# Who forms the block sums of x, and when GpSimd's other sums may run, in a fused attention and SwiGLU kernel

## The chip, the core and the metric

The kernel runs on one core of a Trainium2 chip. The core has a matrix engine (TensorE, PE in the profile), three engines for elementwise work (VectorE is DVE, ScalarE is ACT, GpSimd is POOL) and a queue that issues most transfers (SyncE, SP). Each engine takes its own instructions in the order in which the program wrote them, and waits at an instruction until what it needs is there. The metric is the device time of one execution in microseconds (us); lower is better. A time here is the median of three executions.

## The reference

Attention over keys and values that are averaged over 8 neighbours, and a gated hidden layer on its result:

```python
# q, k, v: (8 batches, 8 heads, 576, 64); Sp = 72 after averaging over 8
k_p = k.reshape(B, H, Sp, 8, D).mean(axis=3)
v_p = v.reshape(B, H, Sp, 8, D).mean(axis=3)
scores = scale * np.matmul(q, k_p.transpose(0, 1, 3, 2))
scores = scores - np.max(scores, axis=-1, keepdims=True)
attn = np.exp(scores)
attn = attn / (np.sum(attn, axis=-1, keepdims=True) + 1e-09)
x = np.matmul(attn, v_p)          # then heads side by side: (4608, 512)
g = x @ w_gate                    # (512, 1536)
silu = g * (1.0 / (1.0 + np.exp(-g)))
out = (silu * (x @ w_val)) @ w_out   # (1536, 512)
```

## The kernel before

**Tiles and steps.** The 4608 rows of x are taken in 9 tiles of 512 (numbered 0 to 8), the 1536 hidden columns in 12 chunks of 128. All fp32 matrices are split in a high and a low half of 16 bits, and a product is three matmuls (high by high, high by low, low by high). For each tile and chunk there is one step: gate and val (512 to 128) into two PSUM banks `gv`, the gate through a tanh (`hf`, L909 on ScalarE), times itself and times val on VectorE (L913, L919), a high half `hh` (L1279, ScalarE) and a low half `hl` (L1285), and the product with w_out (`project`, L931), which adds to four banks `acc`.

**Plain and fast steps.** In a *plain* step gate and val are each 12 matmuls of 512 columns (`side`, L895 to L897). In a *fast* step gate and val are formed together from 7 products of half blocks, 42 matmuls of 256 columns (`product`, L1015). It needs sums of blocks of the weights (`ws_h`, `ws_l`, made once by `fast_weights`) and of x (`fast_x`, the tiles `fx` and `xc`, made in each tile). READY gives the number of fast steps: 0 in tiles 0 and 1, 5 and 7 in tiles 2 and 3, 9 from tile 4 on. The plain steps stand first in a tile, so from tile 4 on there are 3 plain steps and then 9 steps of 7 products.

**The block sums of x.** `fast_x` runs twice in a tile (once for each j of two): VectorE adds the halves of x to `fx` (L980), GpSimd makes four differences of 128x256 (L982 to L985), ScalarE makes the high half (L989), GpSimd the two low halves `xc` (L991). The first fast step of the tile reads all of it.

**What else the engines do.** While a tile's hidden layer runs, the attention of the next rows is prepared: q is split (GpSimd makes the lows, L591), scores are formed (PE, L608), the largest of each row is taken and subtracted (VectorE, L618, L619), the softmax is made, its halves too (GpSimd, L704 and L707), turned by a DMA transpose (SP, L711), multiplied by v (PE, L732 and L733, from the tile `pt`), divided (VectorE, L737), split and turned once more. For each of the 8 batches there are sums of k, v and q ahead of its rows (`prep`): the v sums over 8 run on GpSimd (L283 to L285, three instructions for each of four pieces), the k sums on VectorE (L278), the largest q on VectorE (L339), each after a load into one of three buffers `mid` (issued at L474). GpSimd also makes `hl` in every fast step, VectorE in the plain steps from tile 2 on.

**What sets the order.** The first tile's order is written out by hand. From then on a planner writes it (`hidden_tiles`): between groups of matmuls `slot` offers room, some ns of VectorE and some of ScalarE (ROOM in plain steps, FAST_ROOM in the others), and each line of waiting work (block sums under the name "extra", then the parts of attention and `prep`) goes forward if its stated need fits. The planner keeps a count of how far PE and each engine are; `spend` adds to it and `settle` holds a line until PE's count is past that of the engine. Three constants belong to the count: LANDS (how long after its issue a load is taken to have landed), TURNS (the same for a transpose) and SETTLE (a margin). The count decides only the order: in the run each engine waits for what it really needs. Of the three `mid` buffers, one was also used for the chunks' weights `wf` in the first tile.

Of the kernel before, what the change touches and what calls it, by code (L numbers as in the profile page):

```python
# [8 lines left out]
F16 = mybir.dt.float16  # L9
F32 = mybir.dt.float32  # L10
# [7 lines left out]
P = 128  # L18
# [39 lines left out]
TILE = 512  # L58
SUB = 128


ROOM = (3500, 3500)
FAST = 9
READY = (0, 0, 5, 7, 9)
FAST_ROOM = (3500, 2700), (2850, 2000), (1550, 750), (950, 0), (2300, 500), (2300, 2000), (2600, 4300)
FAST_FIRST, FAST_THEN = 3, 5
ONE_BANK = (1, 8)
LANDS = 5000
SETTLE = 100
TURNS = 3000  # L70
AHEAD = 9


def _plan(nt, s):
# [17 lines left out]
def attention_then_swiglu(  # L92
# [11 lines left out]
    nc = tc.nc  # L104
    B, _, NJ, S = q.shape
# [4 lines left out]
    DM = NJ * P  # L110
# [45 lines left out]
    wo_h = const.tile([P, NCH, DM], F32R, name="wo_h")  # L156
    wo_l = const.tile([P, NCH, DM], BF16, name="wo_l")
    wo_up = wo_h.bitcast(BF16).rearrange("p c (d t) -> p c d t", t=2)[:, :, :, 1]
    ws_h = const.tile([P, FAST, 3, NJ // 2, P], F16, name="ws_h")
    ws_l = const.tile([P, FAST, 3, NJ // 2, P], F16, name="ws_l")  # L160
    p2w = const.tile([P, NCH, 3], F32, name="p2w")
    ones = const.tile([P, P], F32, name="ones")
    nc.gpsimd.memset(ones, 1.0 / UNIT)
# [12 lines left out]
    inv = const.tile([P, B, 3], F32, name="inv")  # L176
    vst_h, vst_l, vst_f = ([vst[:, 2 * n + i] for i in range(2)] for n in range(3))
    halves = [const.tile([P, 2 * H * P], F16, name=f"half{i}") for i in range(2)]
    zeros = const.tile([P, TILE], F16, name="zeros")

    def fields():
        nc.gpsimd.memset(zeros, 0.0)
# [42 lines left out]
            )  # L225

    def w_abs(c):
        wf = chunks[c]["wf"] = mid.tile([P, 3 * DM], F32, name="wf", tag="mid")
        nc.scalar.activation(wf, chunks[c]["high"].bitcast(F32), AF.Abs, scale=2.0**-112)

    def w_join(c):
# [262 lines left out]
    def prep(b):  # L494

        order = 0, 4, 1, 5, 2, 6, 3, 7
        todo = [i for i in order if ("in", b, i) not in state]

        def load():
            if todo and now["loads"] < 2 and not now["hold"] and now["pe"] >= freed[-3]:  # L500
                batch_load(b, todo.pop(0))

        for i in order:
            while i in todo or state["in", b, i] and now["pe"] < state["from", b, i] + LANDS:
                load()
                yield 0, 0
            for n in (0, 1) if i >= 4 else (None,):
                if state["in", b, i]:
                    yield (batch(b, i)[2], 0, "same") if n else (batch(b, i)[2], 0)
                    batch_sum(b, i, n)  # L510
                    load()
        yield from settle("P")
        mx, ks, vs = state["sizes", b]["t"], home["ks"], home["vs"]
        yield 1300, 0
        nc.vector.tensor_reduce(out=mx[:, 0:1], in_=mx[:, 3:7], axis=AX.X, op=ALU.max)
        largest(mx[:, 1:2], ks)
        largest(mx[:, 2:3], vs)
        yield 0, 0
        yield from settle("V")
        while busy["ps"] or (now["one"] and busy["values"]):  # L520
            yield 0, 0
        busy["sums"] = True
        sums = over_rows(mx[:, :3])
        yield 400, 0
        pow2_above(p2s[:, b, :3], inv[:, b], sums)
        yield from settle("V")
        busy["sums"] = False
        nc.vector.tensor_scalar(
            out=p2s[:, b, 3:4], in0=p2s[:, b, 0:1], scalar1=p2s[:, b, 1:2], scalar2=EXPSCALE,
            op0=ALU.mult, op1=ALU.mult,  # L530
        )
        scaled.add(b)
        while b - 2 in under_way:
            yield 0, 0
        for g in range(2):
            yield (1100, 0, "same") if g else (1100, 0)
            split_k(b, g)
        for g in range(2):
            for part in range(4):
                yield 650, 0, "same"  # L540
                split_v(b, g, part)
        prepped.add(b)
# [2 lines left out]
    now = {"one": False, "job": None, "pe": 0, "V": 0, "A": 0, "P": 0, "loads": 0, "hold": False}  # L545

    def spend(engine, n, *after):
        now[engine] = max(now[e] for e in (engine, "pe", *after)) + n

    def settle(*engines, more=SETTLE):  # L550
        end = max(now[e] for e in engines) + more
        while now["pe"] < end:
            yield 0, 0
# [421 lines left out]
    def fast_x(x, xc):  # L975

        for j in range(HJ):
            yield 1400, 0
            f = xp.tile([P, 2, TILE], F32, name="fx", tag="f", bufs=1)
            nc.vector.tensor_add(f, x["h"][:, j::HJ], x["l"][:, j::HJ])  # L980
            b11, b12, b21, b22 = (f[:, i // 2, i % 2 * HT : (i % 2 + 1) * HT] for i in range(4))
            nc.gpsimd.tensor_sub(b11, b12, b11)  # L982
            nc.gpsimd.tensor_sub(b12, b22, b12)
            nc.gpsimd.tensor_sub(b22, b22, b11)
            nc.gpsimd.tensor_sub(b21, b21, b22)  # L985
            spend("P", 3000, "V")
            yield from settle("P")
            yield 0, 1100
            nc.scalar.copy(xc["h"][:, j], f)  # L989
            for i in range(2):  # L990
                nc.gpsimd.tensor_sub(xc["l"][:, j, i], f[:, i], xc["h"][:, j, i])  # L991
            spend("P", 2400, "A")
            yield from settle("P")

    def product(o, k, c, x, xc, begin):

# [260 lines left out]
    def hidden_tiles():  # L1257
# [41 lines left out]
            return t  # L1299

        def keep_fast(t):
            t["rs"] = hp.tile([P, HT], F32, name="rs")
            nc.scalar.copy(t["rs"], t["r"])
            spend("A", 390)

# [12 lines left out]
        for i, (_, n, _) in list(enumerate(tiles))[1:]:  # L1318
# [25 lines left out]
            for at_step, c in enumerate(order):  # L1344
                now["one"] = now["one"] or (i, c) == ONE_BANK
                ends = at_step == 0, at_step == NCH - 1
                now["hold"] = now["hold"] or ends[1]
                following = order[at_step + 1] if not ends[1] else NCH
                soon = following < ready
                hf = hp.tile([P, TILE], F32, name="hf")[:, :n]  # L1350
                new = None
                if fast:
                    t, gate = fast, fast["gate"]
                    if soon:
                        new = begin_fast(following, x, xc)
                    slot(*FAST_ROOM[2])
                    product(gate[:, HT:], 3, c, x, xc, False)
                    tanh(hf, gate, un, c)
                    slot(*FAST_ROOM[3])
                    product(t["x"], 7, c, x, xc, False)  # L1360
                    nc.scalar.copy(t["r"], t["x"])
                    spend("A", 390)
                    gated(hf, gate)
                    nc.vector.tensor_add(t["x"], t["x"], t["rs"])
                    spend("V", 430)
                    if new:
                        keep_fast(new)

                    def fourth():
                        slot(*FAST_ROOM[4])  # L1370
                        if new:
                            seed_fast(new)
                        slot(*FAST_ROOM[5])
                        product(t["r"], 4, c, x, xc, False)
                        times_val(hf, hf, t["val"], un, c)
                        hh = high_of(hf, n)
                        slot(*FAST_ROOM[6])
                        pending.append((acc, *ends, i, c, hh, low_of(nc.gpsimd, hf, hh, n)))

                    def then():  # L1380
                        if new:
                            second_fast(new, following, x, xc)
                        else:
                            slot(*FAST_ROOM[0])

                    flush({NJ + FAST_FIRST: fourth, NJ + FAST_THEN: then})
                    slot(*FAST_ROOM[1])
                else:
                    gate, val = (gv_bank(g, n) for g in range(2))
                    side(x, c, 0, gate, 0, n, lambda: slot(*ROOM))  # L1390
                    tanh(hf, gate, un, c)
                    gated(hf, gate)
                    slot(*ROOM)
                    side(x, c, 1, val, 0, n, lambda: slot(*ROOM))
                    times_val(hf, hf, val, un, c)
                    hh = high_of(hf, n)
                    slot(*ROOM)
                    hl = low_of(nc.gpsimd if i == 1 else nc.vector, hf, hh, n)
                    if c < later:
                        join("extra", fast_weights(c), ("w", c))  # L1400
                    if soon:
                        new = begin_fast(following, x, xc)
                        keep_fast(new)
                        seed_fast(new)
                    flush({NJ: lambda: slot(*ROOM)})
                    if new:
                        second_fast(new, following, x, xc)
                    slot(*ROOM)
                    pending.append((acc, *ends, i, c, hh, hl))
                fast = new  # L1410
# [62 lines left out]
```

## Time and profile before

| what | us |
|---|---|
| median of three executions | 970.64 |
| lowest, highest | 968.14, 971.66 |
| the profiled execution's own time | 976.08 |
| its span on the core | 973.9 |
| PE idle in the span (973.9 less 925.2 busy) | 48.7 |

The mean clock that TensorE was granted over the profiled execution was 0.982 of full speed. In the rows of the profile a start is in microseconds from the start of the span, the number behind it is the duration, then come engine, line, operation and the tiles written and read; brackets hold how long the engine had been idle before that instruction and what released it. Rows on waits have the total, how often, and the longest.

### The profile page before, as it was taken

To read this page: it belongs to the slowest core of one execution; us is meant where nothing else is said; L and a number is where in the kernel's file an instruction comes from. 1 tells how busy PE (TensorE), PEld (TensorE's weight loads), DVE (VectorE), ACT (ScalarE), POOL (GpSimd) and SP (SyncE) were. 2 spreads that over 40 slices of the span, in tenths; PEclk is the share of its full clock that TensorE was granted. 3 is DMA by queue.
4 is the path that set the end of the run, shared out by engine and by line. 5 is a ranking of instruction groups with operands and counts; after the bars stand their busy time and mean duration, and the time that the engine had idled before them with its cause. 6 is when DMAs were issued, how large, how long until landed. Compare 5 with 4: busy or idle time off the path is not lost. (4 is left out here: it accounts for less than half of the span.)

```text
span 973.9 us, 16809 instructions
## 1 busy us (share of the span) xinstructions
PE 925.2 (95%) x6512; PEld 596.2 (61%) x6512; DVE 625.2 (64%) x1097; ACT 495.8 (51%) x971; POOL 470.2 (48%) x531
## 2 busy tenths in 40 slices
PE   5879999999999999999989999899999999999997
PEld 5657555454555575467647764577567757775775
DVE  5788877768967678767667848475754474233223
ACT  2899883355445446444454455435456454333232
POOL 4433336389659655673484337623534353115111
PEclk9799999999999999999989999899999999999999
DMA  9765436256348214941265226712232322001001
GB/s 351 218 172 199 163 109 170 82 161 163 90 112 206 78 40 80 247 101 28 66 197 142 53 49 176 187 43 57 76 71 55 71 66 65 1 1 44 1 1 44
DMA packets 155535, 103.18 MB, mean 106 GB/s; under 512 B 113216, under 2 KB 141888, under 8 KB 153920
## 3 DMA queue, kind: packets, MB, share of 16 engines
q1 hardware_dynamic: 155456, 102.11, 38.6%
q8 instruction: 51, 0.84, 0.4%
q14 instruction: 28, 0.23, 0.1%
HBM read 67.63 MB, written 9.44 MB: 79 GB/s over the span
## 5 line engine op out<-in xcount | busy, mean ns | idle before, releaser
L1285 POOL TENSOR_TENSOR hl<-hf,hh 128x512 bf16<-128x512 f32 x69 | 90.5, 1312 | 216.4 <-ACT hh L1279 216.2
L931 PE MATMUL acc<-hh,wo_l 128*128 128x512 bf16 (+1 forms) x444 | 169.7, 384 | 0.0
L931 PE MATMUL acc<-hl,wo_h 128*128 128x512 bf16 (+1 forms) x444 | 166.9, 378 | 2.9 <-POOL hl L1285 2.5
L909 ACT ACTIVATE hf<-gv,un 128x512 f32<-128x512 f32 (+1 forms) x111 | 74.9, 675 | 185.1 <-PE gv L1015 118.7
L895 PE MATMUL gv<-x,wgv_h 128*128 128x512 f16 (+1 forms) x432 | 159.6, 370 | 4.5 <-DVE hf L913 2.5
L1279 ACT CAST hh<-hf 128x512 fp32r<-128x512 f32 x96 | 59.4, 619 | 201.7 <-DVE hf L919 201.6
L896 PE MATMUL gv<-x,wgv_h 128*128 128x512 f16 (+1 forms) x432 | 159.4, 369 | 1.3 <-DVE x L747 1.3
L897 PE MATMUL gv<-x,wgv_l 128*128 128x512 f16 (+1 forms) x432 | 159.5, 369 | 0.8 <-DVE wgv_l L264 0.8
L913 DVE SCALAR_TENSOR_TENSOR hf<-hf,gv 128x512 f32<-128x512 f32 (+1 forms) x111 | 74.4, 670 | 124.4 <-ACT hf L909 122.2
L931 PE MATMUL acc<-hh,wo_h 128*128 128x512 f32 (+1 forms) x444 | 133.2, 422 | 0.6 <-ACT hh L1279 0.4
L591 POOL TENSOR_TENSOR box<-qt,box 64x512 f16<-64x512 f32 (+1 forms) x60 | 71.6, 1194 | 109.4 <-ACT box L590 79.8
L1015 PEld LDWEIGHTS <-wgv_h 128*128 128x128 f16 x912 | 88.6, 98 | 37.7 <-issue 6.4
L919 DVE SCALAR_TENSOR_TENSOR hf<-gv,un,hf 128x512 f32<-128x512 f32 x96 | 71.6, 746 | 53.3 <-PE gv L1015 40.0
L1015 PE MATMUL gv<-xc,wgv_h 128*128 128x256 f16 x456 | 81.5, 273 | 10.2 <-POOL xc L991 5.4
L931 PEld LDWEIGHTS acc<-hh,wo_h 128*128 128x128 f32 x444 | 78.3, 193 | 16.6 <-ACT hh L1175 0.9
L1015 PE MATMUL gv<-x,wgv_h 128*128 128x256 f16 x456 | 82.5, 276 | 0.0
L1015 PE MATMUL gv<-xc,ws_h 128*128 128x256 f16 x456 | 80.9, 273 | 0.0
L1015 PEld LDWEIGHTS <-ws_h 128*128 128x128 f16 x684 | 66.5, 98 | 23.4 <-issue 1.9
L931 PEld LDWEIGHTS <-wo_h 128*128 128x128 bf16 x444 | 43.7, 98 | 54.5 <-issue 28.6
L897 PEld LDWEIGHTS <-wgv_l 128*128 128x128 f16 x432 | 42.4, 98 | 49.2 <-issue 2.6
L1314 DVE TENSOR_TENSOR gv<-gv,rs 128x256 f32<-128x256 f32 x57 | 24.6, 432 | 72.0 <-PE gv L1015 66.8
L896 PEld LDWEIGHTS <-wgv_h 128*128 128x128 f16 x432 | 42.4, 98 | 45.2 <-issue 6.3
(173 smaller groups left out, 1942.9 us busy)
## 6 DMA issues: line engine op xcount, KB each, us to landing
ws<-w_all SPq DMA_DIRECT2D x12, 1536.0 KB, 7.1
qt<-q_twice SPq DMA_DIRECT2D x48, 256.0 KB, 2.9
out_t<-ob SPq DMA_DIRECT2D x36, 256.0 KB, 2.5
in<-k_rows SPq DMA_DIRECT2D x12, 576.0 KB, 5.3
in<-q_rows SPq DMA_DIRECT2D x12, 576.0 KB, 5.1
in<-v_main SPq DMA_DIRECT2D x12, 512.0 KB, 4.9
in<-v_rest SPq DMA_DIRECT2D x12, 512.0 KB, 4.5
qt<-q_rows SPq DMA_DIRECT2D x8, 256.0 KB, 3.9
```

What stands on the lines that cost most here:

```text
L591: nc.gpsimd.tensor_sub(o[rows], qt[rows], o[rows])
L895: nc.tensor.matmul(o, wh, x["h"][:, j, a:e], start=(j == 0), stop=False)
L896: nc.tensor.matmul(o, wh, x["l"][:, j, a:e], start=False, stop=False)
L897: nc.tensor.matmul(o, wl, x["h"][:, j, a:e], start=False, stop=(j == NJ - 1))
L909: nc.scalar.activation(hf, gate, AF.Tanh, scale=un[:, c, 0:1])
L913: nc.vector.scalar_tensor_tensor(out=hf, in0=hf, scalar=1.0, in1=gate, op0=ALU.add, op1=ALU.mult)
L919: nc.vector.scalar_tensor_tensor(out=out, in0=val, scalar=un[:, c, 2:3], in1=hf, op0=ALU.mult, op1=ALU.mult)
L931: nc.tensor.matmul(acc[j][:, a:e], w[:, c, j * P : (j + 1) * P], h[:, :n], start=begin and at < NJ, stop=end and w is wo_l,)
L1015: nc.tensor.matmul(o, a, b, start=begin and j + n == 0, stop=j == HJ - 1 and n == 2, skip_group_check=True,)
L1279: nc.scalar.copy(hh[:, :n], hf)
L1285: eng.tensor_sub(hl[:, :n], hf, hh[:, :n].bitcast(F32))
L1314: nc.vector.tensor_add(t["gate"][:, HT:], t["x"], t["rs"])
```

## The change

Five things change. (1) *Numbers of the planner*: ROOM, FAST_ROOM, LANDS (5000 to 6250), SETTLE (100 to 0), TURNS (3000 to 4800), and a factor COST in `spend` that takes GpSimd's stated times at 0.92. (2) *Memory*: `ws_h` and `ws_l` become views of one tile `mixed`, which also holds the chunks' `wf` in the first tile, so that `wf` no longer takes a `mid` buffer; `zeros` moves into a buffer of another pool. (3) *`prep`*: a v sum on GpSimd is not issued while a block sum of x is under way. (4) *`fast_x`*: from tile 5 on its differences and lows run on VectorE; in tiles 2 to 4 they stay on GpSimd. (5) *Plain steps from tile 2 on*: the product with val is written back into val's PSUM bank, and high and low are read from there. The number of matmuls is the same.

```diff
-ROOM = (3500, 3500)
+ROOM = (3410, 3290)
...
-FAST_ROOM = (3500, 2700), (2850, 2000), (1550, 750), (950, 0), (2300, 500), (2300, 2000), (2600, 4300)
+FAST_ROOM = (3500, 2400), (3300, 2210), (1250, 1050), (950, 180), (3050, 800), (1460, 3140), (2510, 5200)
...
-LANDS = 5000
-SETTLE = 100
-TURNS = 3000
+LANDS = 6250
+SETTLE = 0
+TURNS = 4800
+COST = (1.0, 1.0, 0.92)
...
-    ws_h = const.tile([P, FAST, 3, NJ // 2, P], F16, name="ws_h")
-    ws_l = const.tile([P, FAST, 3, NJ // 2, P], F16, name="ws_l")
+    mixed = const.tile([P, FAST * 3 * DM // 2], F32, name="mixed")
+    ws_h, ws_l = (
+        mixed.bitcast(F16).rearrange("p (l c k j f) -> p l c k j f", l=2, c=FAST, k=3, j=NJ // 2)[:, i]
+        for i in range(2)
+    )
...
-        wf = chunks[c]["wf"] = mid.tile([P, 3 * DM], F32, name="wf", tag="mid")
+        wf = chunks[c]["wf"] = mixed[:, c % 3 * 3 * DM : (c % 3 + 1) * 3 * DM]
...
-            while i in todo or state["in", b, i] and now["pe"] < state["from", b, i] + LANDS:
+            while (
+                i in todo
+                or state["in", b, i] and now["pe"] < state["from", b, i] + LANDS
+                or i < 4 and any(e["t"][0] == "x" for e in lines["extra"])
+            ):
...
-        now[engine] = max(now[e] for e in (engine, "pe", *after)) + n
+        now[engine] = max(now[e] for e in (engine, "pe", *after)) + n * COST["VAP".index(engine)]
...
-            nc.gpsimd.tensor_sub(b11, b12, b11)
-            nc.gpsimd.tensor_sub(b12, b22, b12)
-            nc.gpsimd.tensor_sub(b22, b22, b11)
-            nc.gpsimd.tensor_sub(b21, b21, b22)
-            spend("P", 3000, "V")
-            yield from settle("P")
+            on = nc.vector if now["tile"] >= 5 else nc.gpsimd
+            pairs = (b12, b11, b11), (b22, b12, b12), (b22, b11, b22), (b21, b22, b21)
+            for at in range(0, 4, 2):
+                if on is nc.vector:
+                    yield 600, 0, "same"
+                for a, b, o in pairs[at : at + 2]:
+                    on.tensor_sub(o, a, b)
+            if on is nc.vector:
+                yield from settle("V")
+            else:
+                spend("P", 3000, "V")
+                yield from settle("P")
...
             for i in range(2):
-                nc.gpsimd.tensor_sub(xc["l"][:, j, i], f[:, i], xc["h"][:, j, i])
-            spend("P", 2400, "A")
-            yield from settle("P")
+                if on is nc.vector:
+                    yield (650, 0, "same") if i else (650, 0)
+                on.tensor_sub(xc["l"][:, j, i], f[:, i], xc["h"][:, j, i])
...
-                    times_val(hf, hf, val, un, c)
-                    hh = high_of(hf, n)
+                    h = hf if i == 1 else val
+                    times_val(h, hf, val, un, c)
+                    hh = high_of(h, n)
                     slot(*ROOM)
-                    hl = low_of(nc.gpsimd if i == 1 else nc.vector, hf, hh, n)
+                    hl = low_of(nc.gpsimd if i == 1 else nc.vector, h, hh, n)
```

The lines of the changed kernel stand a little later than those of before: the differences are L996, the lows L1009, the add L988, `hl` L1306, the lows of the softmax L712 and L715, q's lows L599, the largest q L343.

The first place is GpSimd's queue in tile 4, from the first block sum of x to the end of the second. Before:

```order
L982 TENSOR_TENSOR fx<-fx 128x256
L983 TENSOR_TENSOR fx<-fx 128x256
L984 TENSOR_TENSOR fx<-fx 128x256
L985 TENSOR_TENSOR fx<-fx 128x256
L283 TENSOR_TENSOR in<-in 128x2x256
L284 TENSOR_TENSOR in<-in 128x2x128
L285 TENSOR_TENSOR box<-in 128x128
L704 TENSOR_TENSOR half_129<-sc,half_129 64x8x64
L707 TENSOR_TENSOR half_129<-sc,half_129 64x4x8 x2
L991 TENSOR_TENSOR xc<-fx,xc 128x512 x2
```

And in the changed kernel at the same place:

```order
L996 TENSOR_TENSOR fx<-fx 128x256 x4
L712 TENSOR_TENSOR half_128<-sc,half_128 64x8x64
L715 TENSOR_TENSOR half_128<-sc,half_128 64x4x8 x2
L1009 TENSOR_TENSOR xc<-fx,xc 128x512 x2
L599 TENSOR_TENSOR box<-qt,box 64x4x64 x2
```

The three instructions of a v sum no longer stand between the differences and the lows; the softmax's lows still do.

The second place is VectorE's queue around the second block sum of tile 5. Before (VectorE has only the add L980 of it):

```order
L618 TENSOR_REDUCE mx<-ps 128x4
L619 TENSOR_TENSOR sc<-ps,mx 128x288
L980 TENSOR_TENSOR fx<-x 128x1024
L919 SCALAR_TENSOR_TENSOR hf<-gv_7761,un,hf 128x512
L1285 TENSOR_TENSOR hl<-hf,hh 128x512
L636 TENSOR_REDUCE sm<-sc 128x8
```

And in the changed kernel:

```order
L988 TENSOR_TENSOR fx<-x 128x1024
L996 TENSOR_TENSOR fx<-fx 128x256 x4
L921 SCALAR_TENSOR_TENSOR hf<-hf,gv_7732 128x512
L626 TENSOR_REDUCE mx<-ps 128x4
L627 TENSOR_TENSOR sc<-ps,mx 128x288
L927 SCALAR_TENSOR_TENSOR gv_7733<-gv_7733,un,hf 128x512
L1306 TENSOR_TENSOR hl<-gv_7733,hh 128x512
L626 TENSOR_REDUCE mx<-ps 128x4
L627 TENSOR_TENSOR sc<-ps,mx 128x288
L1009 TENSOR_TENSOR xc<-fx,xc 128x512 x2
```

Four differences and two lows have come to VectorE, with the last plain step's gate, val and low, and two pieces of the scores, between them. The product with val (L927) and its low (L1306) now read a PSUM bank `gv`.

The third place is VectorE's queue in tile 3, where a batch's last pieces of q are reduced to their largest (L339 before, L343 after). Before:

```order
L1364 TENSOR_TENSOR gv_4529<-gv_4529,rs 128x256
L339 TENSOR_REDUCE mx_4375<-in 128x1 x2
L737 TENSOR_TENSOR sc<-ps,ri 128x512
L919 SCALAR_TENSOR_TENSOR hf<-gv_4529,un,hf 128x512
L1314 TENSOR_TENSOR gv_4647<-gv_4587,rs 128x256
```

And in the changed kernel:

```order
L650 RECIPROCAL ri<-sm 128x8
L343 TENSOR_REDUCE mx_4668<-in 128x1 x2
L921 SCALAR_TENSOR_TENSOR hf<-hf,gv_4851 128x512
L1385 TENSOR_TENSOR gv_4783<-gv_4783,rs 128x256
L927 SCALAR_TENSOR_TENSOR hf<-gv_4783,un,hf 128x512
L1335 TENSOR_TENSOR gv_4945<-gv_4907,rs 128x256
```

The division that frees a bank of the scores (L737 before) stood directly behind these reductions and no longer does.

More of the change, by code (lines that the diff above doesn't have):

```diff
@@ L178, in attention_then_swiglu @@
     halves = [const.tile([P, 2 * H * P], F16, name=f"half{i}") for i in range(2)]
-    zeros = const.tile([P, TILE], F16, name="zeros")
+    zeros = hp.tile([P, TILE // 2], F32, name="zeros", tag="rs").bitcast(F16)
     def fields():
@@ L977, in fast_x @@
         for j in range(HJ):
-            yield 1400, 0
+            yield 1200, 0
             f = xp.tile([P, 2, TILE], F32, name="fx", tag="f", bufs=1)
@@ L981, in fast_x @@
             b11, b12, b21, b22 = (f[:, i // 2, i % 2 * HT : (i % 2 + 1) * HT] for i in range(4))
-            nc.gpsimd.tensor_sub(b11, b12, b11)
-            nc.gpsimd.tensor_sub(b12, b22, b12)
-            nc.gpsimd.tensor_sub(b22, b22, b11)
-            nc.gpsimd.tensor_sub(b21, b21, b22)
-            spend("P", 3000, "V")
-            yield from settle("P")
+            on = nc.vector if now["tile"] >= 5 else nc.gpsimd
[10 more added lines that the diff above has]
+                yield from settle("P")
             yield 0, 1100
             nc.scalar.copy(xc["h"][:, j], f)
+            if on is nc.vector:
+                yield from settle("A")
             for i in range(2):
-                nc.gpsimd.tensor_sub(xc["l"][:, j, i], f[:, i], xc["h"][:, j, i])
-            spend("P", 2400, "A")
-            yield from settle("P")
+                if on is nc.vector:
+                    yield (650, 0, "same") if i else (650, 0)
+                on.tensor_sub(xc["l"][:, j, i], f[:, i], xc["h"][:, j, i])
+            if on is nc.vector:
+                yield from settle("V")
+            else:
+                spend("P", 2400, "A")
+                yield from settle("P")
     def product(o, k, c, x, xc, begin):
@@ L1301, in keep_fast @@
         def keep_fast(t):
-            t["rs"] = hp.tile([P, HT], F32, name="rs")
+            t["rs"] = hp.tile([P, HT], F32, name="rs", tag="rs")
             nc.scalar.copy(t["rs"], t["r"])
```

## The prediction

> **What bounds the kernel now.** I read the page first: the busy shares, the chain that ended last, and the table of what PE waited for.
>
> ```profile
> PE 925.2 (95%) x6512; PEld 596.2 (61%) x6512; DVE 625.2 (64%) x1097; ACT 495.8 (51%) x971; POOL 470.2 (48%) x531
> ...
> PE 34%; DVE 2%; DMA 0%; ACT 0%; issue 0%; POOLq 0%; POOL 0%; DVEq 0%
> ```
>
> ```profile
> PE gv L1015 <- POOL xc L991: 5.4, 2, 3.1
> PE gv L1015 <- ACT xc L989: 3.6, 1, 3.6
> ...
> PE acc L931 <- POOL hl L1285: 2.5, 5, 1.2
> PE ps L398 <- DMA vr<-v_main: 2.5, 1, 2.5
> ...
> PE ps L608 <- DVE sc L737: 2.1, 1, 2.1
> ...
> PE ps L732 <- DVE sc L619: 1.3, 1, 1.3
> PE ps L732 <- DMA pt<-half: 1.2, 3, 0.8
> ```
>
> PE is busy for 95% of the span, and the chain names hardly another engine. No matmul is added or removed, so the change can act only through PE's 48.7 us of idle time and through its clock. The largest waits behind the first 100 us are few: the block sums of x (three waits, 9.0 us), the division L737 (2.1). Then I read windows around them (columns: length, busy time of PE, its weight loads, VectorE, ScalarE and GpSimd, granted clock, DMA share, GB/s).
>
> ```profile
> 420.00:440.00 20.00, 17.79 (x141) 12.52 (x139) 11.63 (x21) 6.45 (x14) 13.81 (x17) 0.91 0.33 74
> 500.00:520.00 20.00, 16.67 (x109) 10.80 (x108) 10.11 (x16) 8.59 (x20) 15.15 (x21) 0.83 0.67 170
> 600.00:620.00 20.00, 14.14 (x75) 7.65 (x74) 10.55 (x14) 9.91 (x20) 16.06 (x19) 0.83 0.61 168
> 570.00:585.00 15.00, 13.76 (x107) 9.65 (x106) 8.02 (x18) 8.47 (x19) 5.51 (x7) 1.00 0.20 45
> 479.00:584.80 105.80, 100.82 (x766) 67.98 (x765) 73.12 (x130) 53.59 (x115) 52.89 (x57) 0.97 0.39 102
> 584.80:686.40 101.60, 95.54 (x723) 65.72 (x722) 64.59 (x121) 48.78 (x105) 50.37 (x54) 0.97 0.44 111
> 782.70:876.00 93.30, 92.60 (x691) 63.28 (x690) 43.99 (x77) 37.12 (x77) 29.14 (x29) 1.00 0.15 35
> ```
>
> A long wait costs twice: the clock is 0.83 over the 20 us around each block-sum stall, 17% of 20, so 3.4 us of full speed lost each time, and 0.91 around the wait of 2.1, so 1.8. Around 580, where PE waits 1.24 us, it is 1.00. The last three rows are tiles 4, 5 and 7: they do the same matmuls, the first two take 12.5 and 8.3 us more.
>
> [...]
>
> **The change, part by part.** *Tile 4, sums held back on GpSimd.*
>
> ```profile
> 500.86 1.28 POOL L283 TENSOR_TENSOR in<-in 128x512 f32<-128x512 f32 x1
> ...
> 503.44 1.14 POOL L704 TENSOR_TENSOR half<-sc,half 64x512 f16<-64x512 f32 x1
> ...
> 505.40 2.26 POOL L991 TENSOR_TENSOR xc<-fx,xc 128x512 f16<-128x512 f32 x2
> ```
> ```profile
> 506.60 0.37 PE L1015 MATMUL gv<-xc,wgv_h 128*128 128x256 f16 x1 [3.15 <-POOL xc L991]
> ```
>
> PE waits 3.15 us until the first of the two lows is there. A v sum stands ahead of it on GpSimd, 503.44 less 500.86, 2.6 us, and it goes. Late next are the softmax's lows (1.96 us), which stay: a wait of about 0.5 is left, too short for the clock by the row at 580. Gain 2.65 + 3.4 = 6.05.
>
> *Tile 5, block sums on VectorE.*
>
> ```profile
> 600.54 1.76 POOL L283 TENSOR_TENSOR in<-in 128x512 f32<-128x512 f32 x1
> ...
> 604.46 0.73 POOL L982 TENSOR_TENSOR fx<-fx 128x256 f32<-128x256 f32 x1
> ...
> 611.97 2.27 POOL L991 TENSOR_TENSOR xc<-fx,xc 128x512 f16<-128x512 f32 x2
> ```
> ```profile
> 601.09 2.29 DVE L980 TENSOR_TENSOR fx<-x 128x1024 f32<-128x1024 f16 x1
> ```
> ```profile
> 610.67 0.27 PE L1015 MATMUL gv<-xc,wgv_h 128*128 128x256 f16 x1 [3.63 <-ACT xc L989]
> ...
> 613.18 0.37 PE L1015 MATMUL gv<-xc,wgv_h 128*128 128x256 f16 x1 [2.23 <-POOL xc L991]
> ```
>
> VectorE's add is ready at 603.4, but GpSimd begins the differences at 604.46, behind a v sum, and the lows at 611.97, behind another. On VectorE neither is in the way: 3.63 + 2.23 + 3.4 = 9.26 go, if VectorE has the time. What it takes on:
>
> ```profile
> L1314 DVE TENSOR_TENSOR gv<-gv,rs x57: 422/433/433, 339.4 to 960.5; 128x256 f32<-128x256 f32 x57
> ```
> ```profile
> L1285 DVE TENSOR_TENSOR hl<-hf,hh x27: 632/693/1680, 283.8 to 898.8; 128x512 bf16<-128x512 f32 x27
> ```
> ```profile
> L278 DVE TENSOR_REDUCE box<-in 128x72 f32<-128x576 f32 x24 | 28.2, 1205 | 10.8 <-DMA in<-k_rows 10.8
> L980 DVE TENSOR_TENSOR fx<-x 128x1024 f32<-128x1024 f16 x14 | 20.0, 1431 | 0.0
> ```
> ```profile
> 584.80:607.00 22.20, 22.20 (x152) 11.51 (x151) 18.50 (x34) 11.98 (x24) 16.26 (x17) 1.00 0.68 192
> ```
>
> The trace has no such difference on VectorE; the nearest rows (least, median, most in ns) are L1314 for the same tile and L1285 for the lows. Eight at 0.43 and four at 0.69 make 6.2 us a tile. The last row is tile 5's plain steps, where it must fit: 18.50 + 6.2, less two k sums that the changed order has later (2.4), less 0.9 for the add, which took 2.29 beside GpSimd's sums against a mean of 1.43, is 21.4 of 22.2. It fits with 0.8 us to spare. Bounds: 9.26 won, or all 6.2 laid open on PE. I take the gain, because half the sums' work (the first j) lies two plain steps ahead of its use, and because a piece of attention that is late on VectorE is not what PE needs next. The product kept in PSUM helps a little: both lie on VectorE's and ScalarE's side, off PE's chain, so I count nothing for it (bounds 0, and one step's low late by 0.7).
>
> *The landing at 430.*
>
> ```profile
> 425.72 0.53 SPq L474 DMA_DIRECT2D in<-q_rows  x1
> ```
> ```profile
> 430.76 1.41 DVE L339 TENSOR_REDUCE mx<-in 128x1 f32<-128x576 f32 x2 [3.67 <-DMA in<-q_rows]
> 432.09 0.68 DVE L737 TENSOR_TENSOR sc<-ps,ri 128x512 f32<-128x512 f32 x1
> ```
> ```profile
> 432.82 0.19 PE L608 MATMUL ps<-box 128*128 128x72 f16 x1 [2.10 <-DVE sc L737]
> ```
>
> VectorE sat 3.67 us at a reduction whose load was issued 5.0 us earlier, with the division behind it that frees PE's bank. In the changed order, LANDS being 6250, the reductions come later after their load, and the division does not follow them. Gain 2.1 + 1.8 = 3.9, bounds 0 and 3.9. TURNS at 4800 should take most of the three waits on `pt` (1.2): 1.0, bounds 0 and 2.5, the upper with the wait on L619.
>
> *First tile.*
>
> ```profile
> 31.33 0.49 POOL L285 TENSOR_TENSOR spare<-kr 128x144 f32<-128x144 f32 x1
> ```
> ```profile
> 31.84 0.35 SPq L388 DMA_DIRECT2D vr<-v_main  x1
> ```
>
> The load of v on which PE waits 2.5 us (L398) was issued when GpSimd had released a `mid` buffer (31.82). With `wf` elsewhere a buffer is free, and the issue can follow the one before it on SP, up to 0.9 earlier. I take 0.5, bounds 0 and 0.9. The stalls of the rest of the first 180 us do not involve the change.
>
> *What is added.* The v sums held back run in the fast steps, where GpSimd makes `hl`. A close case is in the trace:
>
> ```profile
> 577.82 2.40 POOL L591 TENSOR_TENSOR box<-qt,box 64x512 f16<-64x512 f32 x2 [7.26 <-ACT box L590]
> ```
> ```profile
> 581.49 0.38 PE L931 MATMUL acc<-hl,wo_h 128*128 128x512 bf16 x1 [1.24 <-POOL hl L1285]
> ```
>
> A block of 2.40 us ahead of `hl` cost PE 1.24, and a v sum is 2.6. Five batches with four such sums each come after tile 2; GpSimd was idle for 52% of the span, and only 5 lows of the trace made PE wait. I count +3, two or three such meetings (bounds 0 and ten meetings, +12.4).
>
> **The sum.** 6.05 + 9.26 + 3.9 + 1.0 + 0.5 = 20.7 gained, 3.0 given back: 17.7. From the profiled 976.08 that is 958.4; the same step from the median 970.64, which is 5.4 lower than the profiled execution, is **953.0 us**.
>
> **Rivals.** *GpSimd's lows are the new wait* (ten meetings, half of the twenty sums): 20.7 − 12.4 = 8.3, so 962.3. For it speaks that a fast step is short, (93.3 − 22.2) / 9 = 7.9 us in tile 7, and takes its low from GpSimd; against, that GpSimd had 52% idle, and the differences it loses from tile 5 on make room.
>
> *The change doesn't do what it says.* The stalls of tiles 4 and 5 merely change their releaser: the softmax's lows (1.96 us) or the cast L989, which stood behind another cast on ScalarE, come as late as the sums did. Then the landing's gain of 3.9 stays, and a little of the waits, less the 3 added: about 968.
>
> *Slower: VectorE becomes the bound in the plain steps of tiles 5 to 7.* It decides when VectorE's idle time there is under the 6.2 us that it takes on; before it was 22.2 − 18.5 = 3.7, so it hangs on what the planner moves out. If nothing does, 6.2 us a tile lie open, and a clock loss of 3.4 with each: 3 × 9.6 = 28.8, less the 20.7, 8 slower: about 979. Against it: the sum above of 21.4 in 22.2, and that the attention's parts on VectorE can run in the fast steps.
>
> [...]
>
> **How the numbers follow.** Chances: the forecast 0.60, GpSimd's lows 0.18, stalls that only move 0.12, VectorE as the bound 0.10. The low end has every term at its upper bound and all waits on `hl` gone: 6.55 + 9.26 + 3.9 + 2.5 + 0.9 + 2.5 = 25.6, so 945, and 1 for the runs' spread: 944. The high end takes in the second case with its bound and reaches towards the third, 967; what lies above is the larger part of the last two cases, under 0.2. By 0.5% (about what a measurement of this kernel can tell from no change) the bounds are 965.8 and 975.5: faster 0.82 (the first two cases and a little of the third), same 0.10, slower 0.08.
>
> **What would show it.** Right: in tiles 4 and 5 the window of 20 us around the first fast step at a clock of 1.00, waits on `xc` under 0.6 us, no wait of scores on the division in tile 3, tiles 4 and 5 near 96. Wrong: PE's waits on `xc` released by VectorE at 2 us or more in tiles 5 to 7; waits on GpSimd's `hl` above 10 us in all; a wait of the first tile that grew, since its order is now another one on SP.

## The result, and the profile after

| what | before | changed |
|---|---|---|
| median, us | 971.15 (4 runs, 968.14 to 973.34) | 945.91 (4 runs, 944.47 to 946.68) |
| ratio | | 0.974, 95% interval 0.9711 to 0.977 |
| profiled execution, us | 976.08 | 944.47 |
| its span; mean granted clock | 973.9; 0.982 | 942.5; 0.994 |

The change saves 25.2 us in the medians and 31.6 between the two profiled executions. Before's profiled execution lies above all four of its timed ones, and its clock is lower than usual: the 40 executions of the kernel before that ran beside the experiments have a median clock of 0.987. The page of the changed kernel, busy shares and the chain that ended last:

```profile
PE 911.6 (97%) x6512; PEld 590.5 (63%) x6512; DVE 635.5 (67%) x1145; ACT 493.5 (52%) x971; POOL 415.1 (44%) x483
...
PE 91%; DMA 3%; DVE 2%; ACT 1%; POOL 1%; issue 1%; SPq 0%; POOLq 0%; DVEq 0%; ACTq 0%
```

PE's idle time went from 48.7 to 942.5 − 911.6 = 30.9 us, so 17.8 of the 31.4 that the span lost were waits. The other 13.6 are PE's own busy time at the same 6512 matmuls: the clock rose by 0.012, which is 11.7 us of 973.9. In the timed executions it rose less, from that 0.987 to 0.993, so an estimate for them is 5.8 of the 25.2 us.

What PE waited for between 100 and 940 us in the changed kernel (total, times, longest):

```profile
PE gv L1036 <- DVE gv L1385: 1.3, 1, 1.3
PE gv L903 <- ACT x L751: 1.1, 1, 1.1
PE gv L904 <- DVE x L755: 0.8, 1, 0.8
PE ps L728 <- DMA pt<-half: 0.5, 1, 0.5
PE acc L939 <- ACT hh L1300: 0.4, 1, 0.4
PE acc L939 <- POOL hl L1306: 0.2, 1, 0.2
```

No row names `xc` or the division, and of the waits on turned softmaxes one of 0.5 is left (L728, a product with v). Where the rest went is read from windows over the start of the program (up to tile 1) and over tiles 3, 4 and 5, with the columns of the prediction. Before:

```profile
0.00:153.20 153.20, 130.81 (x883) 89.84 (x884) 117.86 (x216) 118.37 (x182) 63.65 (x91) 0.96 0.61 197
...
376.80:479.20 102.40, 97.19 (x688) 61.88 (x687) 71.77 (x123) 51.85 (x111) 63.08 (x70) 0.98 0.46 115
479.20:584.80 105.60, 100.62 (x765) 67.89 (x764) 72.92 (x130) 53.59 (x115) 52.89 (x57) 0.97 0.39 102
584.80:686.30 101.50, 95.44 (x722) 65.67 (x721) 64.50 (x120) 48.78 (x105) 50.37 (x54) 0.97 0.44 111
```

The same stages of the changed kernel:

```profile
0.00:151.30 151.30, 129.13 (x883) 87.64 (x884) 117.20 (x216) 118.43 (x182) 63.48 (x91) 0.97 0.62 201
...
371.00:466.50 95.50, 94.16 (x687) 61.03 (x685) 69.32 (x122) 49.38 (x104) 60.55 (x67) 1.00 0.44 118
466.50:562.70 96.20, 96.16 (x759) 65.93 (x758) 68.09 (x129) 52.90 (x115) 51.73 (x58) 1.00 0.46 117
562.70:656.50 93.80, 93.80 (x728) 64.84 (x726) 70.40 (x132) 48.04 (x103) 37.80 (x41) 1.00 0.45 115
```

Tile 3 is 6.9 us shorter, tile 4 9.4, tile 5 7.7: 24.0 of the 31.4, and in tiles 4 and 5 PE is idle for 0.04 us in 190. (The borders of these windows lie up to six matmuls apart in the two kernels.) The start of the program has nearly the same idle time as before, 22.2 against 22.4; its 1.9 us are almost all PE's busy time on the same 883 matmuls, at a clock of 0.97 in place of 0.96.

GpSimd's queue at the second block sum of tile 4, the place that the prediction read:

```profile
484.60 3.14 POOL L996 TENSOR_TENSOR fx<-fx 128x256 f32<-128x256 f32 x4
487.70 1.15 POOL L712 TENSOR_TENSOR half<-sc,half 64x512 f16<-64x512 f32 x1
488.82 0.44 POOL L715 TENSOR_TENSOR half<-sc,half 64x32 f16<-64x32 f32 x2
489.22 2.26 POOL L1009 TENSOR_TENSOR xc<-fx,xc 128x512 f16<-128x512 f32 x2
```

The lows start 1.5 us behind the differences instead of 4.5 (500.86 to 505.40 before). In tile 5, over the plain steps:

```profile
562.70:585.00 22.30, 22.30 (x145) 11.27 (x143) 19.76 (x40) 10.98 (x17) 3.64 (x3) 1.00 0.44 121
```

VectorE is busy for 19.76 of 22.3 and GpSimd for 3.64, where it was 16.26.

### The profile page after: what moved, and what is told of

Its sections match the earlier page's. It is cut to its first block, busy times and chain, and to the rows that moved or that the text cites. A ratio compares the mean times of both kernels' runs of the same rounds, so it can differ in the third digit from the quotient of the medians.

```text
span 942.5 us, 16833 instructions
## 1 busy us (share of the span) xinstructions
PE 911.6 (97%) x6512; PEld 590.5 (63%) x6512; DVE 635.5 (67%) x1145; ACT 493.5 (52%) x971; POOL 415.1 (44%) x483
## 4 chain that ended last, share of the span: by engine, by line
PE 91%; DMA 3%; DVE 2%; ACT 1%; POOL 1%; issue 1%; SPq 0%; POOLq 0%; DVEq 0%; ACTq 0%
PE acc L939 30%; PE gv L1036 28%; PE gv L903 9%; PE gv L904 9%; PE gv L905 9%; DMA kr<-k_rows 1%; PE ps L616 1%; DMA pt<-half 1%; PE ps L740 1%; PE ps L617 1%; PE ps L741 1%; DMA k<-k_rows 1%; DMA in<-q_rows 1%; PE ps L610 1%; ACT ws L227 0%
## 5 line engine op out<-in xcount | busy, mean ns | idle before, releaser
L1306 POOL TENSOR_TENSOR hl<-hf,hh 128x512 bf16<-128x512 f32 x69 | 91.3, 1323 | 235.7 <-ACT hh L1300 235.7
L921 DVE SCALAR_TENSOR_TENSOR hf<-hf,gv 128x512 f32<-128x512 f32 (+1 forms) x111 | 74.2, 669 | 109.4 <-ACT hf L917 108.9
L939 PE MATMUL acc<-hh,wo_h 128*128 128x512 f32 (+1 forms) x444 | 130.5, 416 | 0.6 <-ACT hh L1300 0.4
L599 POOL TENSOR_TENSOR box<-qt,box 64x512 f16<-64x512 f32 (+1 forms) x60 | 68.9, 1149 | 119.2 <-ACT box L598 98.7
L1036 PEld LDWEIGHTS <-mixed 128*128 128x128 f16 x1026 | 99.1, 98 | 26.6 <-issue 1.5
L1036 PEld LDWEIGHTS <-wgv_h 128*128 128x128 f16 x912 | 87.8, 98 | 32.5 <-issue 1.9
L1300 ACT CAST hh<-hf 128x512 fp32r<-128x512 f32 x69 | 42.7, 618 | 115.3 <-DVE hf L927 115.3
L1036 PE MATMUL gv<-xc,mixed 128*128 128x256 f16 x684 | 93.2, 272 | 0.0
L927 DVE SCALAR_TENSOR_TENSOR hf<-gv,un,hf 128x512 f32<-128x512 f32 x69 | 51.5, 746 | 39.1 <-PE gv L1036 35.7
L904 PEld LDWEIGHTS <-wgv_h 128*128 128x128 f16 x432 | 42.2, 98 | 45.1 <-issue 4.4
L903 PEld LDWEIGHTS <-wgv_h 128*128 128x128 f16 x432 | 42.7, 99 | 41.4
```

The costliest lines, as they stand in the source:

```text
L599: nc.gpsimd.tensor_sub(o[rows], qt[rows], o[rows])
L903: nc.tensor.matmul(o, wh, x["h"][:, j, a:e], start=(j == 0), stop=False)
L904: nc.tensor.matmul(o, wh, x["l"][:, j, a:e], start=False, stop=False)
L921: nc.vector.scalar_tensor_tensor(out=hf, in0=hf, scalar=1.0, in1=gate, op0=ALU.add, op1=ALU.mult)
L927: nc.vector.scalar_tensor_tensor(out=out, in0=val, scalar=un[:, c, 2:3], in1=hf, op0=ALU.mult, op1=ALU.mult)
L939: nc.tensor.matmul(acc[j][:, a:e], w[:, c, j * P : (j + 1) * P], h[:, :n], start=begin and at < NJ, stop=end and w is wo_l,)
```

## The experiments

All ratios are to the kernel before, run on the same chip. The parts are numbered as in the section on the change. The first four are the kernel before with one part alone.

**1. Part 3 alone.**

```diff
+                or i < 4 and any(e["t"][0] == "x" for e in lines["extra"])
```

> The kernel before with part 3 alone: GpSimd's v sums are not issued while a block sum of x is under way. By parts: the wait of 3.15 in tile 4 falls to about 0.5 and its 3.4 us of lost clock go; in tile 5 GpSimd also gets its differences and lows without v sums ahead, so of 5.86 + 3.4 most goes too: about 12 us faster, 959. Rival (the new order of everything decides, not the part): the stalls of tiles 4 and 5 shrink but others of 1 us or more appear in other places, and the sum is anything between 960 and 975. Rival (held-back sums cost): waits of PE on GpSimd's lows in the last product rise from 2.5 us in all to 8 or more.

Measured: 965.73 us, ratio 0.9946 (0.9921 to 0.997). Faster by 5.6, about half of what was expected. What PE waited for between 100 and 940 us:

```profile
PE ps L736 <- DMA pt<-half: 4.4, 3, 3.7
PE gv L1019 <- DVE gv L1368: 3.7, 5, 1.9
PE gv L1019 <- ACT xc L993: 3.1, 1, 3.1
PE gv L1019 <- POOL xc L995: 1.6, 2, 1.0
```

The v sum is out of GpSimd's way in tile 4, and PE still waits there, 3.1 for ScalarE's cast and 1.0 for the low behind it. ScalarE's rows show why:

```profile
499.93 0.62 ACT L1283 CAST hh<-hf 128x512 fp32r<-128x512 f32 x1 [2.69 <-DVE hf L923]
500.46 0.50 ACT L592 ACTIVATE qt<-qt,inv 128x256 f32<-128x256 f32 x1
...
501.71 1.03 ACT L993 CAST xc<-fx 128x1024 f16<-128x1024 f32 x1
```

GpSimd's differences were done at 497.5, the cast of them ran at 501.71, behind a step's `hh` and two pieces of q. That is the prediction's third case, a stall that changes its releaser. A wait of 3.7 on a turned softmax in tile 3 is new, and so is one of 1.9 on L1368 in tile 4, as the first rival expected. In tile 5, though, this part alone is enough: of the 5.86 us of waits on `xc` there, 0.5 is left, with GpSimd still making all the sums.

**2. Part 4 alone.** The whole diff of `fast_x`, nothing else; it also asks the planner for 1200 in place of 1400 for the add L980.

> The kernel before with part 4 alone: from tile 5 on the differences and lows of the block sums on VectorE, the product with val in SBUF as before. By parts: tile 5's waits (5.86) and clock (3.4) go, tile 4 keeps its 3.15 and its clock: about 961 to 963. Rival (VectorE is the bound in plain steps without the help of the product in PSUM): waits of PE on xc released by VectorE in tiles 5 to 7, 2 to 6 us each, and a time of 968 to 980.

Measured: 970.68 us, ratio 0.9991 (0.997 to 1.0012): no difference. What PE waited for:

```profile
PE ps L732 <- DMA pt<-half: 5.7, 3, 4.1
PE gv L1028 <- POOL xc L1001: 3.1, 1, 3.1
```

Tile 5's waits on `xc` are gone and tile 4's 3.1 is there, as the parts would have it. But at 610.5 PE waits for a turned softmax instead:

```profile
614.62 0.20 PE L732 MATMUL ps<-box,pt 128*128 128x64 f16 x1 [4.13 <-DMA pt<-half]
```

That transpose was issued at 608.63 here and at 609.15 before. Before, PE came to these products only at 620.79, after the stall on `xc`, which lasted to 613.2, so a late transpose did not show; here it comes to them at 610.5. The transpose itself was also slower, 5.9 us from issue to landing where it was 3.7, which is 2.2 of the 4.1. So the 5.9 us of waiting that were removed came back as 4.1, in part uncovered and in part from the longer transfer. Neither expectation has this; VectorE was not the bound.

**3. Part 1 alone.**

```diff
+ROOM = (3410, 3290)
+FAST_ROOM = (3500, 2400), (3300, 2210), (1250, 1050), (950, 180), (3050, 800), (1460, 3140), (2510, 5200)
+LANDS = 6250
+SETTLE = 0
+TURNS = 4800
+COST = (1.0, 1.0, 0.92)
```

> The kernel before with part 1 alone: ROOM, FAST_ROOM, LANDS, SETTLE, TURNS, COST. By parts: the wait of 2.1 on the division in tile 3 with its clock, and the waits on the turned softmax, go; the stalls of tiles 4 and 5 stay or change by what happens to stand ahead: 966, between 962 and 970. Rival (the numbers carry the change): waits on GpSimd's lows, on scores and in tiles 4 and 5 go as well, and the time is under 957.

Measured: 957.43 us, ratio 0.9854 (0.9819 to 0.989). It is the largest part, faster than the range given for it by parts and just short of the rival's 957. What is left are, above all, the two stalls on the block sums, 2.7 in tile 4 and 2.1 in tile 5, and one low:

```profile
PE gv L1016 <- POOL xc L992: 4.8, 2, 2.7
...
PE acc L932 <- POOL hl L1286: 1.2, 1, 1.2
```

VectorE still sits 2.3 us at a load of q in tile 3 (at 420.30), but no scores wait behind it.

**4. Part 2 alone.** `mixed` and the tag of `zeros`.

> The kernel before with part 2 alone: wf and the weights' block sums in one tile, so that wf takes no buffer of mid. By parts: only the first 100 us change, the wait of 2.5 on v's load becomes 1.6 to 1.9, and with it 0.5 to 1 us: 970, not told from no change. Rival: the first phase gains the 1.9 us that the changed kernel shows up to its tile 1 and the 2.9 behind it, 966.

Measured: 969.02 us, ratio 0.9986 (0.9966 to 1.0005): not told from no change. The wait on v's load is 2.6 in two pieces, the longer 1.6, where it was 2.5 in one.

The next four are the changed kernel with one part undone.

**5. Without part 3.**

```diff
-                or i < 4 and any(e["t"][0] == "x" for e in lines["extra"])
```

> The changed kernel without part 3: v sums may again be issued on GpSimd during a block sum of x. By parts: tile 4 has a wait on xc of 2 to 3 us again, with 3.4 us of clock; tile 5 is on VectorE and stays: about 951 to 952. Rival: the changed numbers keep the v sums out of the way by themselves, no wait on xc over 0.6, 946.

Measured: 953.69 us, ratio 0.9827 (0.9793 to 0.9862), clear of the changed kernel's. GpSimd in tile 4:

```profile
488.14 3.13 POOL L992 TENSOR_TENSOR fx<-fx 128x256 f32<-128x256 f32 x4
...
492.76 1.27 POOL L287 TENSOR_TENSOR in<-in 128x512 f32<-128x512 f32 x1
...
495.33 2.27 POOL L1005 TENSOR_TENSOR xc<-fx,xc 128x512 f16<-128x512 f32 x2
```

The v sum stands between differences and lows again, and PE waits 2.2 us on them. The numbers do not keep it out of the way by themselves. Not all that this run loses belongs to that wait: the clock behind it fell to 0.91 over 20 us, which is 1.8, and the waits on VectorE's L1381 (3.3, against 1.3 on the same statement, L1385, in the changed kernel) and on a low (1.2) came with the other order.

**6. Without part 4**, all block sums on GpSimd.

> The changed kernel without part 4: all block sums on GpSimd again, with v sums held back. By parts: GpSimd without v sums has its differences and lows in time in tile 4, so in tile 5 too, with waits of 0.5 to 2 us: 946 to 951. Rival (GpSimd is too slow for it: four differences of 0.75 and two lows of 1.2 behind the softmax's and q's lows): waits on xc of 2 us or more in each of tiles 5 to 7 with clock losses, 955 to 965.

Measured: 948.24 us, ratio 0.9771 (0.9735 to 0.9807). There is no wait on `xc` in any tile. What it has more than the changed kernel is a wait of 2.0 on GpSimd's low in tile 3, before any sum that was moved; in time it is not told from it. Its edit also puts back the room asked for the add L988, 1400 for 1200, in all tiles, so the order moves ahead of tile 5 too.

**7. Without part 5**, the product with val in SBUF.

> The changed kernel without part 5: the product with val in plain steps goes to SBUF as before, so that its low on VectorE reads two SBUF inputs (mean 847 ns before). By parts: VectorE has 3 x 0.16 us more in the plain steps of a tile, within the 0.8 us to spare: 946 to 947. Rival (the spare time is the point): waits of PE on VectorE's block sums in tiles 5 to 7, 950 to 960.

Measured: 947.1 us, ratio 0.9753 (0.9721 to 0.9784): not told from the changed kernel.

**8. Without part 1**, with the old numbers.

> The changed kernel without part 1: the old ROOM, FAST_ROOM, LANDS, SETTLE, TURNS and no COST. By parts: the landing's wait in tile 3 (2.1 with 1.8 of clock) and those on the turned softmax come back, 950 to 952. Rival (the numbers are what lets the other parts fit): waits on GpSimd's lows and on VectorE's block sums appear, over 6 us in all, and the time is 957 or more.

Measured: 955.63 us, ratio 0.9844 (0.9813 to 0.9874). Between the two theories in time. It has the rival's kind of wait, but not over 6 us of it: 2.5 on VectorE's block sums in tile 5 and 0.6 on lows. The waits on turned softmaxes are there (1.9), but the landing's wait in tile 3 did not come back, and VectorE waits only 0.5 us for q's loads after 150 us:

```profile
PE gv L1035 <- DVE xc L1008: 2.5, 1, 2.5
PE ps L739 <- DMA pt<-half: 1.9, 3, 0.8
```

Four more ask what the first eight left open: whether the engine matters, whether parts 1 and 3 are enough, and what stands behind run 2 and the landing.

**9. The changed kernel with block sums on GpSimd throughout**, the rest of part 4's text kept.

```diff
-            on = nc.vector if now["tile"] >= 5 else nc.gpsimd
+            on = nc.vector if now["tile"] >= 99 else nc.gpsimd
```

> The changed kernel with the new text of the block sums, its 1200 in place of 1400 too, but on GpSimd in all tiles; tiles up to 4 are as in the changed kernel. If the move to VectorE is worth nothing in itself (the kernel without part 4 had no wait on xc, but a wait of 2.0 on GpSimd's low in tile 3, ahead of any moved sum): 946 to 947, no wait on xc over 0.6 in tiles 5 to 7. If the move is what saves the 2.3 us: 948 to 949, with waits of PE in tiles 5 to 7.

Measured: 946.22 us, ratio 0.9756 (0.9717 to 0.9794), like the changed kernel. Its waits up to 940 are nearly the same too, the largest the same 1.3 in tile 3. No difference shows here between the engines that form the sums; run 6's wait in tile 3 came from another order ahead of tile 5.

**10. Parts 1 and 3 on the kernel before.**

> The kernel before with parts 1 and 3 only: block sums on GpSimd, product with val in SBUF, wf in mid. If these two carry the change: 947 to 951, no wait on xc over 1. If VectorE's block sums, the product in PSUM or the memory are needed beside them: 953 to 960, with waits on xc of 2 us or more in tile 4 or 5.

Measured: 951.24 us (946.82 to 955.36), ratio 0.9779 (0.9745 to 0.9814): some 19 of the 25 us, and no wait on `xc`. The profiled execution, the slowest of its four, waits 2.0 on a low and 3.2 on turned softmaxes instead.

**11. Part 4 with LANDS, SETTLE and TURNS.**

> The kernel before with part 4 and only LANDS, SETTLE and TURNS of part 1. Theory: part 4 alone gained nothing because the turned softmax was late by 4.1 us at the same place in tile 5, hidden before under the stall on xc; the larger TURNS puts PE's products with v later, so that wait goes, and with it the landing's 2.3 in tile 3: 958 to 963. Rival: the order falls by chance and other waits of 2 us or more appear: 966 to 972.

Measured: 963.39 us, ratio 0.9915 (0.9889 to 0.9941). The wait on the turned softmax in tile 5 is gone, and so is the landing's in tile 3; the time is just above the range expected of the theory. Tile 4's stall on `xc` has grown from 3.15 to 4.8 (3.1 for ScalarE's cast, 1.7 for GpSimd's low), and VectorE is now late with the block sums of tile 5:

```profile
596.32 0.37 PE L1028 MATMUL gv<-xc,wgv_h 128*128 128x256 f16 x1 [4.62 <-DVE xc L1001]
```

Its queue there (VectorE), and GpSimd's at the same time:

```profile
587.01 3.30 DVE L988 TENSOR_TENSOR fx<-fx 128x256 f32<-128x256 f32 x4
...
591.48 1.17 DVE L278 TENSOR_REDUCE box<-in 128x72 f32<-128x576 f32 x1
...
593.89 1.18 DVE L278 TENSOR_REDUCE box<-in 128x72 f32<-128x576 f32 x1
...
595.58 1.29 DVE L1001 TENSOR_TENSOR xc<-fx,xc 128x512 f16<-128x512 f32 x2
```
```profile
585.96 2.13 POOL L283 TENSOR_TENSOR in<-in 128x512 f32<-128x512 f32 x1 [10.64 <-DMA in<-v_main]
```

Two k sums (2.4 us) lie between differences and lows, and the differences take 3.30 us beside a v sum of GpSimd, where four at 0.43 would be 1.7.

**12. LANDS, SETTLE and TURNS alone.**

```diff
-LANDS = 5000
-SETTLE = 100
-TURNS = 3000
+LANDS = 6250
+SETTLE = 0
+TURNS = 4800
```

> The kernel before with only LANDS, SETTLE and TURNS changed. By the prediction: the wait on the division in tile 3 and its clock (3.9) and about 1 of waits on the turned softmax go: 965 to 967. Rival: these three numbers carry all that part 1 gives (957 alone): 957 to 960. Rival: ROOM, FAST_ROOM and COST carry it: 969 to 972.

Measured: 976.59 us, ratio 1.0056 (1.0036 to 1.0077): slower by 0.56%, which no theory had. PE's waits:

```profile
PE gv L1015 <- ACT xc L989: 5.3, 2, 3.2
PE gv L1015 <- POOL xc L991: 5.2, 2, 3.5
PE gv L895 <- DMA x<-box: 3.6, 1, 3.6
PE ps L608 <- DVE sc L619: 2.5, 2, 2.2
```

The waits on turned softmaxes are small, as meant. The transpose of x itself is late now at tile 5's first step (3.6), and tile 4's stall on `xc` grew from 3.15 to 5.6. The landing's wait in tile 3 has only changed its releaser. VectorE still sits at the reduction of q there:

```profile
414.35 1.41 DVE L339 TENSOR_REDUCE mx<-in 128x1 f32<-128x576 f32 x2 [1.48 <-DMA in<-q_rows]
```

The subtraction L619 now stands behind it in place of the division, and PE's scores wait 2.2 us for that, where it was 2.1.

## Why the prediction was right, and where it was not

The time of 953.0 was 7.1 above what was measured, inside the range, and the likeliest case came: the big waits of tiles 3 to 5 and their clock went. That it came so near is in part luck, since terms were wrong in both directions. Step by step:

- **Tile 4.** Right in its mechanism: run 5 puts the v sum back, and PE waits 2.2 us in that place. With its clock (1.8) that is 4.0 of the 7.8 us that the run loses, against 6.05 forecast. The step that 0.5 would be left was too careful, it is 0. Part 3 does not do it by itself, though: with the old order the cast on ScalarE was late instead (run 1).
- **Tile 5.** The waits and the clock went, and VectorE had the time: 21.4 of 22.2 was worked out, 19.76 of 22.3 measured. The step that failed is the attribution: the 9.26 were put down to the move to VectorE. With GpSimd doing it all, part 3 alone leaves 0.5 of the 5.86 (run 1), and runs 6 and 9 have no wait on `xc`, so it is the v sums out of its way that frees the place. In tiles 4 and 5 together, 17.1 us went between the profiled executions; 15.3 were forecast. (The prediction says that tiles 4, 5 and 7 do the same matmuls; its own rows have 766, 723 and 691.)
- **The clock.** The terms of 3.4, 3.4 and 1.8 were read in a profiled execution with a clock of 0.982, where 0.987 is usual, and then taken off the median.
- **The landing.** The wait and its clock went, but the step that LANDS and TURNS do it failed: with them and SETTLE alone the wait was still there behind another instruction (run 12), and with the old numbers and the other parts it was not (run 8). Part 1 as a whole removes it (run 3). By runs 3 and 12 it hangs on which instruction of VectorE the order puts behind the reductions; which of the numbers make that order is open.
- **First tile.** The forecast 0.5 isn't there: the load's wait fell from 2.5 to 1.9 and that on the gate (L913, now L921) from 2.3 to 1.8, but those on turned softmaxes rose from 2.4 to 3.0 and on a cast of the weights (L244, now L248) from 1.0 to 1.9, so PE's idle time is nearly the same. Waits that grew there were named as a sign of being wrong, and this much of it came. Part 2 alone can't be told from nothing, and the changed kernel without it was not tried.
- **GpSimd's lows.** The term of +3 was mis-sized, in sign too: the waits on `hl` after the first 100 us fell from 2.3 to 0.2. The case was not empty, since runs 6 and 10 each have one such wait of 2.0.
- **The missing time.** Between the profiled executions the span lost 31.4, 13.7 more than the 17.7 forecast. By stages, tiles 4 and 5 gave 1.8 more than forecast, tile 3 3.0 more (waits on L619 there were 1.7 and on lows 0.9, now none), the start 1.4 more. The rest of the program, where 2 were to be lost (the 3.0 for lows less the 1.0 for transposes), gained 5.5. Of this, 2.8 are in tile 1, where the two largest waits are 1.1 and 0.8 in both kernels, but the clock over 160 to 180 us was 0.91 before and is 1.00 now; the last section shows how PE's idle time lay there.
- **The slower rival** did not come in the changed kernel, and it is not decided by VectorE's time alone. VectorE was late by 4.6 us in run 11, where two k sums lie in the way, and by 2.5 in run 8, where none does. In run 2 it took two k sums in the plain steps and was not late. What runs 8 and 11 share is a late start: the add of the second block sum began 5 to 6 us ahead of tile 5's first fast step (584.36 and 590.74 in run 8, 585.76 and 590.93 in run 11), against 11 in the changed kernel (574.70 and 585.47) and 12 in run 2 (593.21 and 604.99).

The parts do not add. Alone, parts 3, 4, 1 and 2 give 5.6, 0.6, 13.9 and 2.3 us, the second and the last not told from nothing; part 5 alone was not tried. Undone, parts 3, 4, 5 and 1 cost 7.8, 2.3, 1.2 and 9.7, and only the first and the last of these stand clear of the changed kernel's interval. (These medians come from sessions in which the kernel before itself had medians from 970.6 to 972.5, so a microsecond says little.) Parts 1 and 3 are needed; of 2, 4 and 5 none is shown to be. No variant was faster than the changed kernel.

## What to carry to other kernels

Before a stall is priced, look for what would be late behind it: in run 2 PE waited 4 us for a transpose at the place where a stall of 6 us had gone, and removing the stall alone gained nothing. Where a planner sets the order, a part's gain is the gain in one particular order; undo parts of the end state as well as adding them one by one, and ask whether the place of the work, not its engine, was the fault. Where a wait of some two microseconds goes, read the clock as well: around the division's 2.1 us it was 0.91 over 20 us before, around the 2.02 of run 6 it was 1.00. Between the profiled executions the clock was over a third of the gain (11.7 of 31.4), in the timed ones, by the estimate above, nearer a quarter.

## What the runs showed of the hardware

Some instructions of VectorE took longer beside GpSimd. In the changed kernel (least, median, most in ns):

```profile
L996 DVE TENSOR_TENSOR fx<-fx x32: 424/426/1379, 564.1 to 856.6; 128x256 f32<-128x256 f32 x32
L1009 DVE TENSOR_TENSOR xc<-fx,xc x16: 679/682/1162, 570.4 to 859.5; 128x512 f16<-128x512 f32 x16
L1306 DVE TENSOR_TENSOR hl<-gv,hh x27: 674/690/702, 279.0 to 867.5; 128x512 bf16<-128x512 f32 x27
```

The differences have both inputs in SBUF: the four that overlap with work of GpSimd take 1371 to 1379 ns, the other 28 take 424 to 426. `hl`, which with two SBUF inputs reached 1680 ns before, stays at 702 with one in PSUM, though 16 of its 27 overlap with work of GpSimd. Ahead of the one stall that is left in the changed kernel's tile 3 there is such an instruction too. VectorE there:

```profile
439.01 2.50 DVE L649 TENSOR_SCALAR sm<-sm 128x8 f32<-128x8 f32 x1
```

and GpSimd:

```profile
438.69 1.15 POOL L712 TENSOR_TENSOR half<-sc,half 128x512 f16<-128x512 f32 x1
...
440.21 1.27 POOL L1306 TENSOR_TENSOR hl<-hf,hh 128x512 bf16<-128x512 f32 x1
```

Eight numbers a row, at most 0.17 us in the four cases without GpSimd beside them, take 2.50 us and end as GpSimd's run of work ends (441.48). PE then waits 1.34 us for L1385, which stands behind it on VectorE after a reciprocal, two reductions of q and L921, so the 2.3 us lost cover that stall. What held the instruction up beside GpSimd's, the trace does not show.

Whether a wait of 2 us cost the clock was not decided by its length here. The same wait on GpSimd's low in tile 3 was 2.01 us in run 10 and 2.02 in run 6, and the clock fell behind the first alone (0.91 over 425 to 445 us, against 1.00 over 422 to 442). The traces record when the clock was at half. In the profiles of before and of the changed kernel these stretches (8 and 4) begin at whole multiples of 3.41 us from one another, and up to 940 us each lasts 3.41 or 6.83. Two windows of this grid in run 10, then two in run 6 (length, then PE's busy time; the clock is the third number from the end):

```profile
430.54:433.95 3.41, 1.40 (x11) 0.92 (x10) 0.84 (x2) 1.35 (x3) 3.33 (x4) 1.00 0.56 120
433.95:437.36 3.41, 3.41 (x17) 2.12 (x15) 0.75 (x1) 2.34 (x4) 3.33 (x5) 0.50 0.97 356
```
```profile
427.40:430.81 3.41, 1.68 (x10) 1.06 (x11) 0.68 (x2) 0.95 (x2) 3.33 (x4) 1.00 0.65 167
430.81:434.23 3.42, 3.42 (x30) 2.75 (x29) 2.26 (x4) 2.34 (x4) 3.34 (x6) 1.00 1.00 358
```

In run 10 the whole wait lies in one window, which is idle for 2.01 us, and the next is at half clock. In run 6 it begins before the line at 427.40, so the window has 1.73 us of idle time, and the clock stays. The two profiles fit. Between 100 and 940 us, four windows at full clock were followed by one at half clock, all before the change, with 2.08, 2.10, 2.31 and 3.14 us of idle PE; of the windows that were not, none had more than 1.56 before and 1.88 in the changed kernel. So in these traces the clock stayed behind 1.88 us of idle time in a window of 3.41 and fell behind 2.01 (roughly, since the ends of matmuls in a trace are modelled), and one window at 0.50 loses 1.7 us of full speed.

The windows do not begin at the same times in the two profiles: one begins at 171.26 us before and one at 170.12 in the changed kernel. PE's idle time around the two waits of tile 1 (1.1 and 0.8 in both) fell almost whole into that window before, 2.08 us, and is split in the changed kernel into 0.56 and 1.88. So the clock that was won in tile 1 goes with where the idle time lay in the windows, not with shorter waits; whether the change or chance put it there was not shown.
